# The last 128 columns of the last tile, stored as two transfers of 64 rows from two queues

## The chip, the cores and the metric

The kernel runs on one core of a Trainium2 chip. The core's engines are TensorE (PE, with its weight loads PEld), VectorE (DVE), ScalarE (ACT), GpSimd (POOL) and SyncE (SP); they run on their own and meet through semaphores. Sixteen DMA engines carry the transfers that SyncE and ScalarE issue here, each from a queue of its own (q1 and q10 in the profile). The metric is the device time of one execution in microseconds.

## The reference

One mixer block: a layer norm and a first product with GELU, a shift of the four quarters of its columns by one or two rows of the sequence, a second product, a residual, then a second layer norm and a two-layer MLP with another residual.

```python
B, S, D, F = 1, 2048, 512, 1792          # all inputs bfloat16
def reference(x, w1, w2, w3, w4):
    h = _gelu(_layernorm(x, axis=-1) @ w1)
    c = D // 4
    g0 = jnp.pad(h[:, :, 0*c:1*c], ((0, 0), (1, 0), (0, 0)))[:, :S, :]
    g1 = jnp.pad(h[:, :, 1*c:2*c], ((0, 0), (0, 1), (0, 0)))[:, 1:, :]
    g2 = jnp.pad(h[:, :, 2*c:3*c], ((0, 0), (2, 0), (0, 0)))[:, :S, :]
    g3 = jnp.pad(h[:, :, 3*c:   ], ((0, 0), (0, 2), (0, 0)))[:, 2:, :]
    hs = jnp.concatenate([g0, g1, g2, g3], axis=-1) @ w2
    x1 = x + hs
    h2 = _gelu(_layernorm(x1, axis=-1) @ w3) @ w4
    return x1 + h2
```

## The kernel before

The 2,048 rows of the sequence are held as 16 tiles of 128 rows, one row of a tile per partition: row 16p + t is partition p of tile t, so one partition's part of the output is 16 rows that follow each other, and one tile's store writes 128 pieces that lie 16 rows apart. Everything stays on chip between the two layers.

Operations are recorded one by one with `add(engine, name, function, reads, writes, dma)`. `arrange` then orders them: each engine has a list of names that come first, written out by hand, and all others follow in the order in which they were recorded. `emit` walks the ordered operations, works out for each which semaphores it must wait for, and gives every DMA a semaphore of its own that it raises by 16 when it has landed. At the end of SyncE's program it waits for every store (the operations whose names begin with `out`), line 168 and 169. When the program is built, these waits are put together two to an instruction, and one that is left over is held by the branch that ends SyncE's part (L92).

The first layer and the mixing (L357 to L494) take about the first 48 us, with a first part of the second layer's products (L526) among them. In the second layer the tiles go in four groups of four: `block3` (L502, with GELU on ScalarE, L513) makes the hidden activations of a group, and `m4` (L545) multiplies one tile of 128 rows by `w4`, 14 matmuls one after the other into one PSUM bank. `fin` (L553) adds the residual on VectorE (L557) into `o_sb`, a ring of four output tiles, and issues the store (L561), on SyncE unless told otherwise. Group 1 is computed ahead of group 0's second product, and so on, so that the last stretch is the second products of groups 2 and 3: eight tiles, and nothing but these.

The last tile (line 760) is cut in two by columns: 384 columns into bank 0 with a store on SyncE, then 128 columns into bank 7 with a store on ScalarE. ScalarE has no other work in this stretch: the slices of the page show it idle over the last 20 us and more. The last store's chain is thus: last matmul, addition of 128 x 128 on VectorE, issue on ScalarE's queue, transfer of 128 pieces of 256 B, landing, the wait on SyncE, and the barrier of all engines at the end.

Four helpers in the same function, `nbias_op`, `norm_act`, `negmean` and `norm_pool`, are not called by anything that runs: the only call stands behind `if t in ():` (line 624), which is never true. The two small tensors that they use, `nmean` and `nbias`, are allocated.

Of the kernel before, what the change touches and what calls it, by code (L numbers as in the profile page):

```python
# [5 lines left out]
P = 128  # L6
ACT_F = mybir.ActivationFunctionType
ALU = mybir.AluOpType
BF16 = mybir.dt.bfloat16
F32 = mybir.dt.float32  # L10
# [16 lines left out]
class Program:  # L27
# [7 lines left out]
    def add(self, eng, name, fn, reads=(), writes=(), dma=False):  # L35
        self.ops.append(Op(name, eng, fn, reads, writes, dma))
# [135 lines left out]
def bass_standalone__mixer_s_mlp__prompt_kernel(nc: bass.Bass, x, w1, w2, w3, w4, out):  # L172
    B, S, D = x.shape
    F = w3.shape[1]
    assert (B, S, D, F) == (1, 2048, 512, 1792)
    NT = S // P
# [7 lines left out]
    od = out[0].rearrange("(p t) d -> p t d", t=NT)  # L184
    ORDER = [(t + R + 2) % NT for t in range(NT)]
    POS = {t: k for k, t in enumerate(ORDER)}

    with ExitStack() as es:
        sb = lambda name, shape, dt: es.enter_context(nc.sbuf_tensor(name, shape, dt))
# [17 lines left out]
        st9 = sb("st9", [P, 2 * NT, 9], F32)  # L207
        mv = sb("mv", [P, 2 * NT, 2], F32)
        rstd = sb("rstd", [P, 2 * NT], F32)
        nmean = sb("nmean", [P, 2 * NT], F32)  # L210
        nbias = sb("nbias", [P, 2 * NT], F32)
        neghalf = sb("neghalf", [P, 4], F32)
        warm = sb("warm", [P, 1], F32)
        o_sb = sb("o_sb", [P, 4, D], BF16)
# [32 lines left out]
        add = pr.add  # L247
# [4 lines left out]
        def bres(b, n, tag):  # L252
            return [(("ps", b + i), tag) for i in range(n)]
# [28 lines left out]
        def src_of(layer, t):  # L282
            return (x_sb, ("x", t)) if layer == 0 else (x1_sb, ("x1", t))

        def dst_of(layer, t):
            return (xn, t, ("xn", t), 0) if layer == 0 else (x1n, POS[t] % 8, ("x1n", POS[t] % 8), t)
# [19 lines left out]
        def norm(layer, t):  # L306
            src, r = src_of(layer, t)
            dst, k, dr, tag = dst_of(layer, t)
            i = layer * NT + (t if layer == 0 else POS[t])
            add("dve", f"nm{layer}_{t}",  # L310
                lambda e: e.tensor_scalar(dst[:, k, :], src[:, t, :], mv[:, i, 0:1], rstd[:, i : i + 1],  # L311
                                          ALU.subtract, ALU.mult),
                reads=[(r, 0), (("mv", i), 0), (("rstd", i), 0)], writes=[(dr, tag)])

        def nbias_op(layer, t, n):
            i = layer * NT + (t if layer == 0 else POS[t])
            add("dve", f"nb{layer}_{t}",
                lambda e: e.scalar_tensor_tensor(nbias[:, i : i + n], mv[:, i : i + n, 0], -1.0,
                                                 rstd[:, i : i + n], ALU.mult, ALU.mult),
                reads=[(("mv", i + k), 0) for k in range(n)] + [(("rstd", i + k), 0) for k in range(n)],  # L320
                writes=[(("nb", i + k), 0) for k in range(n)])

        def norm_act(layer, t):
            src, r = src_of(layer, t)
            dst, k, dr, tag = dst_of(layer, t)
            i = layer * NT + (t if layer == 0 else POS[t])
            add("act", f"na{layer}_{t}",
                lambda e: e.activation(dst[:, k, :], src[:, t, :], ACT_F.Identity,
                                       bias=nbias[:, i : i + 1], scale=rstd[:, i : i + 1]),
                reads=[(r, 0), (("nb", i), 0), (("rstd", i), 0)], writes=[(dr, tag)])  # L330

        def negmean(layer, t, n):
            i = layer * NT + (t if layer == 0 else POS[t])
            add("dve", f"ng{layer}_{t}",
                lambda e: e.tensor_scalar(nmean[:, i : i + n], mv[:, i : i + n, 0], -1.0, None, ALU.mult),
                reads=[(("mv", i + k), 0) for k in range(n)], writes=[(("nmean", i + k), 0) for k in range(n)])

        def norm_pool(layer, t):
            src, r = src_of(layer, t)
            dst, k, dr, tag = dst_of(layer, t)  # L340
            i = layer * NT + (t if layer == 0 else POS[t])
            add("pool", f"np{layer}_{t}",
                lambda e: e.tensor_scalar(dst[:, k, :], src[:, t, :], nmean[:, i : i + 1], rstd[:, i : i + 1],
                                          ALU.add, ALU.mult),
                reads=[(r, 0), (("nmean", i), 0), (("rstd", i), 0)], writes=[(dr, tag)])


        def tp(t, n, b, raw):
# [192 lines left out]
        def m4(q, i, b, c0=0, c1=D, part=""):  # L541
            def f(e):
                ins = None
                for fc in range(FC):
                    ins = e.matmul(ps[:, 512 * b : 512 * b + c1 - c0], h2T[:, fc, q % 2, P * i : P * (i + 1)],  # L545
                                   w4_sb[:, fc, c0:c1], start=(fc == 0), stop=(fc == FC - 1))
                return ins

            add("pe", f"m4_{q}_{i}{part}", f,
                reads=[("w4", 0)] + [(("h2T", fc, q % 2, i // 2), q) for fc in range(FC)],  # L550
                writes=bres(b, 1, f"m4_{q}_{i}{part}"))

        def fin(q, i, b, c0=0, c1=D, part="", eng="sp"):  # L553
            k = 4 * q + i
            t = ORDER[k]
            add("dve", f"fin{t}{part}",
                lambda e: e.tensor_tensor(o_sb[:, k % 4, c0:c1], ps[:, 512 * b : 512 * b + c1 - c0],  # L557
                                          x1_sb[:, t, c0:c1], ALU.add),
                reads=bres(b, 1, f"m4_{q}_{i}{part}") + [(("x1", t), 0)], writes=[(("o", k % 4, c0), k)])
            add(eng, f"out{t}{part}",  # L560
                lambda e: e.dma_start(od[:, t, c0:c1], o_sb[:, k % 4, c0:c1]),  # L561
                reads=[(("o", k % 4, c0), k)], dma=True)

        def warmup(name, n, b):
            def f(e):
# [55 lines left out]
        for t in range(R, NT, 2):  # L621
            roots(0, t, 2)
        for t in range(R, NT):
            if t in ():
                nbias_op(0, t, 1)
                norm_act(0, t)
            else:
                norm(0, t)
        for t in range(R, NT, 2):
            if t in (8, 10):  # L630
                tp(t, 2, 6 + t // 2 % 2, False)
# [112 lines left out]
        for i, t in enumerate((0, 1, 2, 3, 4, 5, 6, 7)):  # L744
            b = (6, 7, 1)[i % 3]
# [3 lines left out]
        for i in range(4):  # L749
            m4(0, i, 6 + i % 2)  # L750
            fin(0, i, 6 + i % 2)
        block3(2)
        for i in range(4):
            m4(1, i, 6 + i % 2)
            fin(1, i, 6 + i % 2)
        block3(3)
        for q in (2, 3):
            for i in range(4):
                b = 6 + i % 2
                if (q, i) == (3, 3):  # L760
                    m4(q, i, 0, 0, 384, "a")
                    m4(q, i, 7, 384, 512, "b")
                    fin(q, i, 0, 0, 384, "a")
                    fin(q, i, 7, 384, 512, "b", eng="act")
                else:
                    m4(q, i, b)
                    fin(q, i, b)
# [32 lines left out]
```

## Time and profile before

| | us |
|---|---|
| median of three runs | 136.84 (136.6 to 136.96) |
| the profiled execution | 136.96 |
| its span in the profile | 134.9 |
| TensorE busy | 131.4 (97%) |
| VectorE busy | 58.0 (43%) |
| ScalarE busy | 46.7 (35%) |
| GpSimd busy | 12.5 (9%) |
| additions of `fin`, L557 | 17 of 0.66 on average |
| stores of 128 KB on SyncE, issue to landing | 15, median 1.8 |

The span runs from the first to the last instruction of the program; the execution's own time has some 2 us around it. The granted clock of TensorE is at full speed throughout. Busy shares are averages over the whole span: in the last 25 us TensorE works without a break, VectorE adds once per tile, ScalarE is idle, and the DMA engines move one store of 128 KB in about 3 us. A DMA's "issue" is the time that its instruction takes on the engine that issues it; its "landing" is when the sixteenth step of its semaphore arrives.

### The profile page before, as it was taken

How to read it: one execution, taken by the hardware profiler on the slowest of the kernel's cores; microseconds unless marked ns; L12 is line 12 of the kernel's file. 1: busy time of each engine (PE TensorE's matmuls, PEld its weight loads, DVE VectorE, ACT ScalarE, POOL GpSimd, SP SyncE). 2: the span in 40 equal slices, each digit the busy share in tenths (PEclk: the TensorE clock that was granted, in tenths of full speed). 3: DMA queues.
4: the chain of work that ended last, by engine and by line, in shares of the span. 5: the costliest groups of instructions: out<-in, count | busy, mean ns of one | idle time of the engine just before them, and what ended most of it. 6: DMA issues, size and time to landing. Idle time of an engine off the chain costs nothing.

```text
span 134.9 us, 1809 instructions
## 1 busy us (share of the span) xinstructions
PE 131.4 (97%) x729; PEld 69.5 (52%) x729; DVE 58.0 (43%) x135; ACT 46.7 (35%) x56; POOL 12.5 (9%) x25
## 2 busy tenths in 40 slices
PE   7989999999999999999999999999999999999993
PEld 2346866668885444444444444444444444444452
DVE  0399999799966786772222000122200002322222
ACT  3467871607963025551000555200066630000000
POOL 2024422220321012220000000000000000000000
PEclk9999999999999999999999999999999999999999
DMA  4998569985455993444112000011110001111121
GB/s 116 311 234 171 184 128 236 266 274 114 77 110 106 261 306 67 88 80 78 39 50 67 5 0 0 0 39 39 39 39 5 0 0 39 39 39 39 41 76 43
DMA packets 24568, 12.96 MB, mean 96 GB/s; under 512 B 16752, under 2 KB 23920, under 8 KB 24560
## 3 DMA queue, kind: packets, MB, share of 16 engines
q1 hardware_dynamic: 23984, 12.42, 36.0%
q10 hardware_dynamic: 576, 0.43, 1.1%
q8 instruction: 6, 0.10, 0.3%
q14 instruction: 2, 0.02, 0.1%
HBM read 6.82 MB, written 2.10 MB: 66 GB/s over the span
## 4 chain that ended last, share of the span: by engine, by line
PE 93%; DMA 3%; SPq 2%; issue 0%; DVE 0%
PE ps L545 36%; PE ps L502 27%; PE ps L526 9%; PE ps L444 6%; PE ps L484 5%; PE ps L470 5%; PE ps L412 3%; DMA x_sb<-in_x_dram 3%; PE ps L357 1%; SPq L274 1%; SPq L576 1%; DVE o_sb L557 0%; PE ps L400 0%
## 5 line engine op out<-in xcount | busy, mean ns | idle before, releaser
L545 PE MATMUL ps<-w_sb,h2T 128*128 128x512 bf16 (+2 forms) x238 | 48.9, 366 | 0.0
L557 DVE TENSOR_TENSOR o_sb<-ps,x_sb 128x512 bf16<-128x512 f32 (+2 forms) x17 | 11.2, 660 | 61.2 <-PE ps L545 61.2
L513 ACT ACTIVATE h2T<-ps 128x1024 bf16<-128x1024 f32 x21 | 21.5, 1023 | 46.2 <-PE ps L502 46.2
L502 PE MATMUL ps<-x1nT,w_sb 128*128 128x512 bf16 x168 | 36.7, 379 | 0.0
L545 PEld LDWEIGHTS ps<-w_sb,h2T 128*128 128x128 bf16 x238 | 22.8, 98 | 25.9
L502 PEld LDWEIGHTS ps<-x1nT,w_sb 128*128 128x128 bf16 x168 | 16.4, 98 | 19.8
L291 DVE BATCH_NORM_STATS2 st<-x_sb 128x6 f32<-128x512 bf16 x32 | 20.7, 679 | 4.6 <-DMA x_sb<-in_x_dram 4.5
L302 POOL TENSOR_TENSOR rstd<-mv,neghalf 128x2 f32<-128x2 f32 x16 | 11.6, 726 | 46.5 <-DVE mv L296 46.5
L526 PE MATMUL ps<-x1nT,w_sb 128*128 128x256 bf16 x112 | 12.4, 273 | 0.0
L526 PEld LDWEIGHTS ps<-x1nT,w_sb 128*128 128x128 bf16 x112 | 11.0, 98 | 1.5
L494 DVE TENSOR_TENSOR x_sb<-ps,x_sb 128x512 bf16<-128x512 f32 x16 | 10.6, 686 | 2.5 <-PE ps L470 1.5
L444 PE MATMUL ps<-xnT,w_sb 128*128 128x256 bf16 x80 | 9.2, 273 | 0.0
L537 ACT ACTIVATE h2T<-ps 128x1024 bf16<-128x1024 f32 (+1 forms) x8 | 7.1, 914 | 6.0 <-PE ps L526 6.0
L444 PEld LDWEIGHTS ps<-xnT,w_sb 128*128 128x128 bf16 x80 | 7.7, 98 | 1.2
L311 DVE TENSOR_SCALAR x1n<-x_sb,mv,rstd 128x512 bf16<-128x512 bf16 x16 | 5.9, 410 | 5.3 <-POOL rstd L302 5.3
L484 PE MATMUL ps<-w_sb,hTf 128*128 128x512 bf16 x32 | 7.2, 379 | 0.0
L470 PE MATMUL ps<-w_sb,hTf 128*128 128x512 bf16 x32 | 7.1, 379 | 0.0
L412 PE MATMUL ps<-w_sb,xnT 128*128 128x512 bf16 x24 | 6.0, 386 | 0.0
L454 ACT ACTIVATE hTf<-ps 128x1024 bf16<-128x1024 f32 x4 | 4.1, 1023 | 4.1 <-PE ps L444 4.1
L366 ACT ACTIVATE xnT<-ps 128x512 bf16<-128x512 bf16 (+1 forms) x6 | 4.4, 737 | 2.9 <-PE ps L357 2.9
L296 DVE BATCH_NORM_AGGREGATE mv<-st 128x2 f32<-128x9 f32 x32 | 5.0, 186 | 0.0
L470 PEld LDWEIGHTS ps<-w_sb,hTf 128*128 128x128 bf16 x32 | 3.1, 98 | 3.6
(28 smaller groups left out, 36.7 us busy)
## 6 DMA issues: line engine op xcount, KB each, us to landing
out_dram<-o_sb SPq DMA_DIRECT2D x15, 128.0 KB, 1.8
w_sb<-in_w_dram SPq DMA_DIRECT2D x1, 1792.0 KB, 7.8
x_sb<-in_x_dram SPq DMA_DIRECT2D x13, 128.0 KB, 3.4
w_sb<-in_w_dram SPq DMA_DIRECT2D x4, 256.0 KB, 4.2
w_sb<-in_w_dram SPq DMA_DIRECT2D x6, 128.0 KB, 3.1
w_sb<-in_w_dram SPq DMA_DIRECT2D x4, 192.0 KB, 3.5
w_sb<-in_w_dram ACTq DMA_DIRECT2D x2, 128.0 KB, 3.3
x_sb<-in_x_dram SPq DMA_DIRECT2D x1, 256.0 KB, 4.3
```

What stands on the lines that cost most here:

```text
L291: add("dve", f"st{layer}_{t}", lambda e: e.bn_stats(st9[:, i, 0:6], src[:, t, :]), reads=[(r, 0)], writes=[(("st6", i), 0)])
L302: lambda e: e.tensor_tensor(rstd[:, i : i + n], mv[:, i : i + n, 1], neghalf[:, 0:n], ALU.pow),
L412: ins = e.matmul(bank(b), xnT[:, t, c, :], w1_sb[:, c, :], start=(c == 0), stop=(c == DC - 1))
L444: ins = e.matmul(dst, w1_sb[:, c, P * fc : P * (fc + 1)], xnT[:, t : t + 2, c, :], start=(c == 0), stop=(c == DC - 1))
L470: ins = e.matmul(bank(b), hTf[:, c0 : c0 + P], w2_sb[:, j, :], start=(j == 0), stop=(j == DC - 1))
L484: ins = e.matmul(bank(b), hTf[:, w[0] : w[0] + P], w2_sb[:, j, :], start=first and n == 0, stop=last and n == len(js) - 1)
L494: lambda e: e.tensor_tensor(x1_sb[:, t, :], bank(b), x_sb[:, t, :], ALU.add),
L502: ins = e.matmul(bank(b), w3_sb[:, c, P * fc : P * (fc + 1)], x1nT[:, 4 * q : 4 * q + 4, c, :], start=(c == 0), stop=(c == DC - 1))
L513: lambda e: e.activation(h2T[:, fc : fc + 2, q % 2, :], src, ACT_F.Gelu_apprx_tanh),
L526: ins = e.matmul(dst, w3_sb[:, c, P * (fc + i) : P * (fc + i + 1)], x1nT[:, t : t + 2, c, :], start=(c == 0), stop=(c == DC - 1))
L545: ins = e.matmul(ps[:, 512 * b : 512 * b + c1 - c0], h2T[:, fc, q % 2, P * i : P * (i + 1)], w4_sb[:, fc, c0:c1], start=(fc == 0), stop=(f ...
L557: lambda e: e.tensor_tensor(o_sb[:, k % 4, c0:c1], ps[:, 512 * b : 512 * b + c1 - c0], x1_sb[:, t, c0:c1], ALU.add),
```

## The change

`fin` takes a tuple of engines in place of one. For n engines it records n stores, each of 128 / n partitions of the same columns, on the engines in turn, all behind the same addition. The calls that gave no engine give `("sp",)` by default and make one store as before. The last call, for 128 columns of the last tile, gives `("act", "sp")`: partitions 0 to 63 are stored from ScalarE's queue, 64 to 127 from SyncE's. The stores are 18 in place of 17, so SyncE has one semaphore more to wait for at the end. The four unused helpers, their tensors and the branch that is never taken are removed.

```diff
-        nmean = sb("nmean", [P, 2 * NT], F32)
-        nbias = sb("nbias", [P, 2 * NT], F32)
...
-        def nbias_op(layer, t, n):
...
-        def norm_act(layer, t):
...
-        def negmean(layer, t, n):
...
-        def norm_pool(layer, t):
...
-        def fin(q, i, b, c0=0, c1=D, part="", eng="sp"):
+        def fin(q, i, b, c0=0, c1=D, part="", eng=("sp",)):
             k = 4 * q + i
             t = ORDER[k]
             add("dve", f"fin{t}{part}",
                 lambda e: e.tensor_tensor(o_sb[:, k % 4, c0:c1], ps[:, 512 * b : 512 * b + c1 - c0],
                                           x1_sb[:, t, c0:c1], ALU.add),
                 reads=bres(b, 1, f"m4_{q}_{i}{part}") + [(("x1", t), 0)], writes=[(("o", k % 4, c0), k)])
-            add(eng, f"out{t}{part}",
-                lambda e: e.dma_start(od[:, t, c0:c1], o_sb[:, k % 4, c0:c1]),
-                reads=[(("o", k % 4, c0), k)], dma=True)
+            for n, e in enumerate(eng):
+                p0, p1 = P * n // len(eng), P * (n + 1) // len(eng)
+                add(e, f"out{t}{part}{n}",
+                    (lambda p0, p1: lambda e: e.dma_start(od[p0:p1, t, c0:c1], o_sb[p0:p1, k % 4, c0:c1]))(p0, p1),
+                    reads=[(("o", k % 4, c0), k)], dma=True)
...
-            if t in ():
-                nbias_op(0, t, 1)
-                norm_act(0, t)
-            else:
-                norm(0, t)
+            norm(0, t)
...
-                    fin(q, i, 7, 384, 512, "b", eng="act")
+                    fin(q, i, 7, 384, 512, "b", eng=("act", "sp"))
```

More of the change, by code (lines that the diff above doesn't have):

```diff
@@ L313, in norm @@
                 reads=[(r, 0), (("mv", i), 0), (("rstd", i), 0)], writes=[(dr, tag)])
-        def nbias_op(layer, t, n):
[L316 to L321, printed above, removed]
-        def norm_act(layer, t):
[L324 to L330, printed above, removed]
-        def negmean(layer, t, n):
[L333 to L336, printed above, removed]
-        def norm_pool(layer, t):
[L339 to L345, printed above, removed]
         def tp(t, n, b, raw):
```

## The prediction

> **What bounds the kernel now.** I read the chain of waits first, then the timeline of the last three microseconds, then the same stretch cut into windows with the share of the DMA engines.
>
> ```profile
> span 134.9 us, 1809 instructions
> PE 93%; DMA 3%; SPq 2%; issue 0%; DVE 0%
> ```
>
> TensorE carries 93% of the chain that ended last, in one piece from the first transposes to the last matmul. Nothing in the diff is an instruction of TensorE, so only what follows its last matmul can move. The timeline from 131.9 us (start, length, engine and line):
>
> ```profile
> 131.69 0.89 PE L545 MATMUL ps<-w_sb,h2T 128*128 128x128 bf16 x13
> 131.84 0.56 DVE L557 TENSOR_TENSOR o_sb<-ps,x_sb 128x384 bf16<-128x384 f32 x1 [1.58 <-PE ps L545]
> 132.42 0.33 SPq L561 DMA_DIRECT2D out_dram<-o_sb  x1
> 132.62 0.29 DVE L557 TENSOR_TENSOR o_sb<-ps,x_sb 128x128 bf16<-128x128 f32 x1 [0.22 <-PE ps L545]
> 132.94 0.35 ACTq L561 DMA_DIRECT2D out_dram<-o_sb  x1
> ```
>
> The reader is to see the order: matmuls end at 132.58, the last addition runs 132.62 to 132.91, ScalarE issues the last store at 132.94, and SyncE has been free since 132.75. The windows of the tail (stretch, length, busy per engine, then clock, DMA share, GB/s) show what that store does next:
>
> ```profile
> 133.70:133.79 0.09, 0.00 (x0) 0.00 (x0) 0.00 (x0) 0.00 (x0) 0.00 (x0) 1.00 0.00 0
> 133.79:134.07 0.28, 0.00 (x0) 0.00 (x0) 0.00 (x0) 0.00 (x0) 0.00 (x0) 1.00 0.55 117
> 134.07:134.42 0.35, 0.00 (x0) 0.00 (x0) 0.00 (x0) 0.00 (x0) 0.00 (x0) 1.00 0.00 0
> 134.42:134.88 0.46, 0.00 (x0) 0.00 (x0) 0.00 (x0) 0.00 (x0) 0.00 (x0) 1.00 0.00 0
> ```
>
> So of the 1.94 us from the issue to the end of the span, 0.85 us pass before the first packet (132.94 to 133.79), 0.28 us move data, 0.35 us pass from the last packet to the landing, and 0.46 us are SyncE's last waits and the closing barrier. Rows of the DMA view by size, and the packets of ScalarE's queue (q10) after 132.9 us:
>
> ```profile
> out_dram<-o_sb SPq DMA_DIRECT2D x15, 128.0 KB, 1.8
> out_dram<-o_sb SPq DMA_DIRECT2D x1, 96.0 KB, 1.7
> out_dram<-o_sb ACTq DMA_DIRECT2D x1, 32.0 KB, 1.5
> q10 hardware_dynamic: 144, 0.03, 7.4%
> ```
>
> Four times the bytes add only 0.3 us to a landing. The 144 packets are 128 rows of 256 B and 16 small ones, one for each DMA engine. The final waits, from the view of L169 before and after 134.05:
>
> ```profile
> L169 SPq EVENT_SEMAPHORE  x6: 28/28/28, 132.8 to 133.1; - x6
> L169 SPq EVENT_SEMAPHORE  x2: 28/28/28, 134.1 to 134.4; - x2
> ```
>
> Each of these waits holds for two stores. Six of them, long satisfied, take 0.3 us for five steps, so 0.06 us each; the seventh waits for the 96 KB store, the eighth for the last one, and the seventeenth store's is held by the branch behind them (L92).
>
> **The change part by part.** *Removed code.* Four helper functions and a branch that is never taken go, with two small tensors: 2 x 32 x 4 B = 256 B per partition. The instructions of TensorE, VectorE and GpSimd are the same in number, form and order, so I put this at 0.00 us. No cover is needed, since no instruction goes.
>
> *Issue on ScalarE.* Its store has 64 rows in place of 128, still behind the same addition, so it starts at 132.94. The duration does not follow the rows: the 1,792 KB load on SyncE takes 0.58 us for 1,792 runs of 1 KB, the stores 0.33 for 128. I take 0.35 us as before, 0.00 in the sum.
>
> *Issue on SyncE.* One more issue, which waits for the same addition. Queued behind it on SyncE are only the final waits, and only the closing barrier waits for those. SyncE ended its 96 KB issue at 132.75; six loads issued back to back from 2.12 us take 2.80 us together and the last of them 0.43, so (2.80 - 0.43) / 5 = 0.47 us from start to start, and it could start again at 132.42 + 0.47 = 132.89, ahead of 132.91. It starts with ScalarE's, at about 132.93, and ends at 133.27. Its early waits then run from about 133.3 to 133.7 (six of 0.06 us), still ahead of the landing of the 96 KB store at 134.08, where SyncE stops today too. So 0.00, hidden by that flight; without the cover the 0.33 us would stand in front of the end.
>
> *From issue to first packet.* SyncE's 96 KB store takes 0.83 us (132.42 to 133.25), ScalarE's 0.85. What the trace of the tail doesn't show is two issues at one moment. The only such pair opens the kernel:
>
> ```profile
> 0.74 0.39 SPq L274 DMA_DIRECT2D x_sb<-in_x_dram  x1
> 0.74 0.89 ACTq L576 DMA_DIRECT2D w_sb<-in_w_dram  x2
> ```
>
> In the trace's packet records SyncE's queue moves its first packet at 1.77 us, 1.03 after its issue, and ScalarE's at 2.04, 1.30 after. Bounds for the later half: 0.00 (the tail's own rows) to 1.30 - 0.85 = +0.45. The pair is two reads of 128 KB at a cold start, the tail's are writes of a quarter of that or less, so I take 0.00 and keep +0.45 for the range.
>
> *Data.* The 128 rows of 256 B are spread as before over the 16 engines, 4 + 4 for each in place of 8, and 32 small packets stand in place of 16. Busy share 0.55 of 0.28 us is 0.15 us for each engine, so its engines start one after the other within the rest, about 0.13 us. If the two queues halve both parts, 0.28 becomes 0.14: -0.14. If they only interleave on the same engines: 0.00, with one more small packet of at most 0.01. By size (0.3 us for 96 KB more) 16 KB less would be worth 0.3 x 16/96 = 0.05. I take 0.00, since both halves end on the same engines, and keep -0.14 and +0.01.
>
> The Trainium skill, DMA: Bandwidth & Descriptors, section Rules for kernel authors, advises against just this: two transfers to disjoint partition halves share the same 16 engines and serialize, and one of 128 partitions is to be used. By that rule the gain of 0.14 is not there; by the size row alone it would be 0.05. The trace of before has no pair of halves that would decide.
>
> *Landing.* 0.35 us from the last packet, one row, taken unchanged: 0.00. The fifteen full stores land within 0.1 us of each other but for one of 2.3 us, which had an instruction fetch on one engine at 130.5; none is near the last store.
>
> *One more final wait.* Seventeen stores become eighteen: the first wait is now for one store alone, then eight pairs, then the branch. The last two event waits are for SyncE's half and for ScalarE's half. When both land together, the second is passed 0.06 us after the first where today only one stands there: +0.06. SyncE's first packet comes 0.02 us sooner after its issue, so its half lands sooner by about that and I take 0.06 - 0.02 = +0.04. Bounds: 0.00 (it lands 0.06 ahead) and +0.06.
>
> *Sum.* 0.00 + 0.00 + 0.00 + 0.00 + 0.04 = +0.04 us: a span of 134.88 + 0.04 = 134.92, and 136.96 + 0.04 = 137.00 for the profiled execution, whose own time of 136.96 has 2.08 us around the span. It is the slowest of the three runs shown, 0.12 above the median of 136.84, so the forecast for the median is 136.88, **136.9**. Differences under 0.3%, 0.41 us, are about what a measurement of this kernel cannot tell from no change: the three runs alone spread over 0.36.
>
> **The rivals.** *The halves run side by side.* Data 0.28 to 0.14, the extra wait +0.04: 136.84 - 0.14 + 0.04 = 136.74. For it: two queues, and engines that now start one after the other within 0.28 us. Against it: each queue's 64 rows go over all 16 engines. It can't reach far: even with no data at all, 0.85 + 0.35 of 1.48 us stay, a gain of 0.28 at most (136.56).
>
> *The two issues hold each other up before their first packets* (slower). The place is the 0.85 us between issue and first packet, the price that of the kernel's first pair, 0.45 us for ScalarE's queue: 136.84 + 0.45 = 137.29; SyncE's half is then long landed and the extra wait costs nothing. It decides for "slower" from 0.41 us. For it: in that pair ScalarE's first packet comes 0.27 us after SyncE's though both were issued at 0.74. Against it: both are late there, as a cold start would make them, and 0.27 alone (137.1) would not show.
>
> *SyncE comes late*, so the halves aren't issued together. An issue after a wait can take 0.58 us (the 1,792 KB load) in place of 0.33: a half later by 0.25 us, 136.84 + 0.25 = 137.09. Against it: all sixteen stores on SyncE took 0.33 to 0.36, and each had waited too.
>
> **How the numbers follow.** Interleaved halves with an extra wait 0.57 (136.9), side by side 0.17 (136.7), held up 0.20 (137.1 to 137.3), SyncE late 0.06 (137.1). Slower by over 0.41 us: the upper end of held up, 0.13, and 0.03 from the scatter of a median of a few runs on the others, 0.16 in all. Faster by over 0.41 lies beyond the floor of 0.28, so it needs scatter: 0.07. Within: 0.77. The range runs from 136.5 (the floor of 136.56 less some scatter) to 137.3 (held up at its full price); about 15 in 100 lie outside.
>
> **What would show it.** Right: two issues of 64 rows at 132.93 to 132.95 against 132.94 for one, both queues' packets within one stretch of about 0.28 us that begins 0.85 after, both landings within 0.05 us, nine final waits in place of eight, with the last two 0.06 apart, and the matmuls ending at the same distance from the start. Held up: a gap between the first packets of q1 and q10, or both over 0.9 us after their issues. Side by side: a stretch of 0.14 us. Wrong altogether: a shift ahead of 132.9 us, an instruction fetch in the tail, or a landing over 0.5 us after the last packet.

## The result and the profile after

The changed kernel is slower: a median of 137.46 us against 136.84, a ratio of 1.0044 (95% interval 1.0029 to 1.0058), so between 0.40 and 0.79 us slower. Its profiled execution took 137.32 us, with a span of 135.13. The head of its page and its chain:

```profile
span 135.1 us, 1811 instructions
PE 89%; SPq 4%; DMA 2%; DVE 2%; issue 0%
```

The two new instructions are one store and one final wait. TensorE's smaller share of the chain is a difference in the first 12 us, where the chain now goes by SyncE's loads and a layer norm's statistics, and it cost nothing: the long run of TensorE behind it begins 0.35 us earlier than in the profiled execution of before (the first block of 32 matmuls at 14.55 us against 14.90), and so do the last additions. That much differs between executions (in the profiles shown here the last addition ends between 132.5 and 133.3 us), so I compare the tail, from the end of the last addition to the end of the span. Before it was 134.88 - 132.91 = 1.97 us. The timeline after (start, length, engine and line):

```profile
131.49 0.56 DVE L523 TENSOR_TENSOR o_sb<-ps,x_sb 128x384 bf16<-128x384 f32 x1 [1.58 <-PE ps L511]
132.07 1.07 SPq L529 DMA_DIRECT2D out_dram<-o_sb  x2
132.27 0.29 DVE L523 TENSOR_TENSOR o_sb<-ps,x_sb 128x128 bf16<-128x128 f32 x1 [0.22 <-PE ps L511]
132.59 0.56 ACTq L529 DMA_DIRECT2D out_dram<-o_sb  x1
```

The addition ends at 132.56, so the tail is 135.13 - 132.56 = 2.57 us, 0.60 longer; the medians differ by 0.62. All of the change in time is behind the last addition. ScalarE's issue takes 0.56 us in place of 0.35. SyncE's row merges two issues: 0.33 for 384 columns and, from 132.59, 0.56 for the half. The windows of the tail, with the DMA share and GB/s at the end of a line, then the issues and the packets after 132.5 us:

```profile
133.36:133.78 0.42, 0.00 (x0) 0.00 (x0) 0.00 (x0) 0.00 (x0) 0.00 (x0) 1.00 0.00 0
133.78:134.30 0.52, 0.00 (x0) 0.00 (x0) 0.00 (x0) 0.00 (x0) 0.00 (x0) 1.00 0.38 63
134.30:134.68 0.38, 0.00 (x0) 0.00 (x0) 0.00 (x0) 0.00 (x0) 0.00 (x0) 1.00 0.00 0
134.68:135.14 0.46, 0.00 (x0) 0.00 (x0) 0.00 (x0) 0.00 (x0) 0.00 (x0) 1.00 0.00 0
```

```profile
q1 hardware_dynamic: 224, 0.11, 16.4%
q10 hardware_dynamic: 80, 0.02, 3.9%
issues: line engine op xcount, KB each, median us to landing
out_dram<-o_sb SPq DMA_DIRECT2D x1, 16.0 KB, 1.8
out_dram<-o_sb ACTq DMA_DIRECT2D x1, 16.0 KB, 2.1
```

The two halves land 1.8 and 2.1 us after their issues; the whole took 1.5. The first packet comes 133.79 - 132.59 = 1.20 us after the start of the issues, and the stretch with data is 0.52 us long in place of 0.28. In the packet records SyncE's 64 rows run from 133.79 to 134.02 and ScalarE's from 134.06 to 134.30: one queue after the other, not between each other. The final waits before and after 133.7 us:

```profile
L169 SPq EVENT_SEMAPHORE  x6: 17/28/28, 133.2 to 133.5; - x6
L169 SPq EVENT_SEMAPHORE  x3: 28/28/28, 133.7 to 134.7; - x3
```

Nine waits, six of them early and over by 133.55, as forecast. The last one starts when ScalarE's half has landed (134.67), and from there to the end it is 0.46 us, as before.

### The profile page after: what moved, and what is told of

Same layout as the page of the kernel before. It is cut to its first block, busy times and chain, and to the rows that moved or that the text cites. A ratio compares the mean times of both kernels' runs of the same rounds, so it can differ in the third digit from the quotient of the medians.

```text
span 135.1 us, 1811 instructions
## 1 busy us (share of the span) xinstructions
PE 131.2 (97%) x729; PEld 69.1 (51%) x729; DVE 58.0 (43%) x135; ACT 46.8 (35%) x56; POOL 12.5 (9%) x25
## 4 chain that ended last, share of the span: by engine, by line
PE 89%; SPq 4%; DMA 2%; DVE 2%; issue 0%
PE ps L511 36%; PE ps L468 27%; PE ps L492 9%; PE ps L410 6%; PE ps L436 5%; PE ps L450 5%; DMA x_sb<-in_x_dram 2%; SPq L272 2%; SPq L351 1%; DVE st L289 1%; PE ps L323 1%; SPq L544 1%; DVE xn L309 0%; DVE o_sb L523 0%
```

## The experiments

Each was made from the changed kernel. "Tail" is as above, from each one's profile; ratios are to the kernel before, run on the same chip. "First packet" is read from the packet records, counted from the issue's start.

**One whole store again.**

```diff
-                    fin(q, i, 7, 384, 512, "b", eng=("act", "sp"))
+                    fin(q, i, 7, 384, 512, "b", eng=("act",))
```

> The changed kernel with its last store whole again (128 rows on ScalarE's queue); the removed helpers and tensors stay removed. Theory (two issues at one moment hold each other up): the tail, from the end of the last addition to the end of the span, is 1.97 us as before (2.57 in the changed kernel), the issue 0.35, and the median is that of before, 136.8 to 136.9. Rival (the removed tensors or the new line numbers matter): the median stays near 137.46.

The tail is 1.96 us, the median 136.66, the ratio 0.9991 (0.9979 to 1.0004). The timeline and the issue:

```profile
132.52 0.35 ACTq L529 DMA_DIRECT2D out_dram<-o_sb  x1
```

The removed helpers and tensors are worth nothing that can be measured; the loss is in the split of one store.

**One half alone.**

```diff
             for n, e in enumerate(eng):
                 p0, p1 = P * n // len(eng), P * (n + 1) // len(eng)
+                if e is None:
+                    continue
...
-                    fin(q, i, 7, 384, 512, "b", eng=("act", "sp"))
+                    fin(q, i, 7, 384, 512, "b", eng=("act", None))
```

> Leaves out the store of rows 64 to 127 of the last 128 columns; ScalarE's store of rows 0 to 63 stays and no other is issued at its moment. Theory (simultaneous issues): issue 0.35 us, first packet 0.85 after it, tail 1.9 to 1.97 us, median 136.8. Rival (a transfer of 64 rows is slow by itself): issue 0.56, first packet 1.2 or more, tail 2.3 or more, median 137.2 or more.

The rival held. With no other issue at its moment the half still takes 0.54 us to issue, and its first packet comes after 1.18 us in place of 0.85. Timeline, then its landing:

```profile
132.93 0.54 ACTq L531 DMA_DIRECT2D out_dram<-o_sb  x1
```

```profile
out_dram<-o_sb ACTq DMA_DIRECT2D x1, 16.0 KB, 1.8
```

Tail 2.26 us, 0.29 more than before; median 137.25, ratio 1.0028 (1.0013 to 1.0042). About half of the loss is a price of the transfer of 64 rows itself.

**Halves by columns.**

```diff
-                p0, p1 = P * n // len(eng), P * (n + 1) // len(eng)
+                a0, a1 = c0 + (c1 - c0) * n // len(eng), c0 + (c1 - c0) * (n + 1) // len(eng)
                 add(e, f"out{t}{part}{n}",
-                    (lambda p0, p1: lambda e: e.dma_start(od[p0:p1, t, c0:c1], o_sb[p0:p1, k % 4, c0:c1]))(p0, p1),
+                    (lambda a0, a1: lambda e: e.dma_start(od[:, t, a0:a1], o_sb[:, k % 4, a0:a1]))(a0, a1),
```

> The last 128 columns as two stores of 128 rows x 64 columns, from ScalarE and SyncE at the same moment. Theory (simultaneous issues, whatever the rows): issues 0.56 us each, the first packets of the two queues 0.27 apart, tail 2.57 to 2.7 us, median 137.4 to 137.6. Rival (64 rows are slow): issues 0.33 and 0.35, tail 2.0 us, median 136.9.

Neither. Two issues at one moment, of 128 rows each, take 0.33 and 0.37 us (0.85 in SyncE's row are two issues 0.52 apart):

```profile
132.29 0.85 SPq L529 DMA_DIRECT2D out_dram<-o_sb  x2
...
132.82 0.37 ACTq L529 DMA_DIRECT2D out_dram<-o_sb  x1
```

```profile
out_dram<-o_sb SPq DMA_DIRECT2D x1, 16.0 KB, 1.4
out_dram<-o_sb ACTq DMA_DIRECT2D x1, 16.0 KB, 1.6
```

SyncE's half lands a little sooner than the whole (1.4 against 1.5), ScalarE's later: its first packet 0.06 us later, and 0.49 us in place of 0.35 from its last packet to its landing. Tail 2.11, 0.14 more than before; median 137.03, ratio 1.0016 (1.0005 to 1.0026). So two transfers issued at one moment have a price of their own, and my theory had put all of the loss on it.

**Which queue, or which rows.**

```diff
-                    fin(q, i, 7, 384, 512, "b", eng=("act", "sp"))
+                    fin(q, i, 7, 384, 512, "b", eng=("sp", "act"))
```

> Two halves of 64 rows at one moment, but SyncE stores rows 0 to 63 and ScalarE rows 64 to 127. Theory: as the changed kernel, issues 0.56 us, one queue's first packet 0.27 after the other's, tail 2.57, median 137.4 to 137.5; which queue comes second does not follow the rows. Rival (the rows decide, through the partitions that are read): rows 64 to 127 come first as in the changed kernel, so now ScalarE's queue is first.

Tail 2.58 us, median 137.26, ratio 1.0037 (1.0021 to 1.0053). SyncE's half is again the first (landing 1.8 us after its issue) and ScalarE's the second (2.1), its first packet 0.28 us after SyncE's. SyncE's issue starts 0.005 us ahead of ScalarE's in both kernels. The rows don't decide.

**Every tile in halves of 64 rows.** The same pair at the end, and fifteen pairs in the body, where matmuls hide them.

```diff
-            fin(0, i, 6 + i % 2)
+            fin(0, i, 6 + i % 2, eng=("act", "sp"))
...
-            fin(1, i, 6 + i % 2)
+            fin(1, i, 6 + i % 2, eng=("act", "sp"))
...
-                    fin(q, i, b)
+                    fin(q, i, b, eng=("act", "sp"))
```

> Every output tile, not only the last part, is stored as two halves of 64 rows from ScalarE and SyncE at one moment: fifteen pairs hidden behind matmuls, and the pair at the end as in the changed kernel. Theory (a transfer of 64 rows costs its issue and its start each time): all issues about 0.55 us, the first packets of the two queues about 0.27 apart in every pair, the tail 2.57 us, the median 137.4. Rival (only the first transfer of a new shape on a queue is slow): the first pair 0.55, the later ones 0.33 to 0.37, the tail 2.0 to 2.15, the median about 137.0.

The issues in the view by line (shortest, median, longest in ns; SyncE's shortest is the store of 384 columns):

```profile
L529 SPq DMA_DIRECT2D out_dram<-o_sb x17: 366/467/557, 63.9 to 133.0; - x17
L529 ACTq DMA_DIRECT2D out_dram<-o_sb x16: 497/498/557, 63.9 to 133.0; - x16
```

Both had a part of it. The first pair takes 0.557 us on each queue, all later ones 0.467 and 0.498, so 0.06 to 0.09 is paid only once; the rest is paid each time. The first packets of the two queues are 0.28 to 0.30 us apart (issue to first packet 1.12 on SyncE, 1.42 on ScalarE) in every later pair, for rows of 1 KB and of 256 B alike. So the second queue doesn't wait for the end of the first one's data: with rows of 1 KB SyncE's data last 0.46 to 0.47 us, and ScalarE's packets begin before they end. The tail is 2.89 us, which here holds something else: 0.89 us lie behind the last landing in place of 0.46. The waits and the branch behind them:

```profile
L169 SPq EVENT_SEMAPHORE  x16: 28/28/28, 133.5 to 135.0; - x16
L92 SPq COMPARE_BRANCH  x1: 38/38/38, 135.5 to 135.5; - x1
```

The waits don't make the difference: all but the last are over when the last half lands (134.97), and the last starts 0.02 us later. But the branch starts only 0.49 us after the last wait, 0.07 in the changed kernel, though the store that it waits for had landed at 65.9. The median, 137.47, ratio 1.0037 (1.0017 to 1.0057), can therefore not be read against the changed kernel's; the packets can.

**Every tile in halves of columns.** The edit of the column halves with that of the run before.

> As the run before, but the parts of every pair are 128 rows by half of the columns, at the end too. Theory (two issues at one moment cost little where each has 128 rows): issues 0.33 and 0.35 to 0.38 us, ScalarE's first packets 0.06 to 0.1 after SyncE's, ScalarE's landing 0.1 to 0.2 later than alone, tail 2.11, median 137.0. Rival (the shared engines make the second of two wait for the first one's data): the second queue's first packet comes later the wider the rows are, over 0.2 us after the first queue's in the body's pairs of 256 columns.

Issues 0.33 and 0.37 us as expected. ScalarE's first packet comes 0.17 us after SyncE's for rows of 512 B (0.12 in the first pair) and 0.08 for the 128 B at the end, so the second queue does wait longer behind wider rows, though not 0.2. ScalarE's landings are 0.16 us later than SyncE's. Tail 2.48, of which 0.87 are behind the last landing, with the same late branch as in the run before; median 137.27, ratio 1.0019 (1.0003 to 1.0035).

**Other numbers of rows, one transfer at a time.**

```diff
+            cuts = [0, (64, 32, 96, 16, 112, 64, 32, 96, 16, 112, 64, 32, 96, 16, 112)[k], P] if len(eng) == 2 else [0, P]
             for n, e in enumerate(eng):
-                p0, p1 = P * n // len(eng), P * (n + 1) // len(eng)
+                p0, p1 = cuts[n], cuts[n + 1]
...
-            fin(0, i, 6 + i % 2)
+            fin(0, i, 6 + i % 2, eng=("sp", "sp"))
...
-            fin(1, i, 6 + i % 2)
+            fin(1, i, 6 + i % 2, eng=("sp", "sp"))
...
-                    fin(q, i, 7, 384, 512, "b", eng=("act", "sp"))
+                    fin(q, i, 7, 384, 512, "b", eng=("act",))
...
-                    fin(q, i, b)
+                    fin(q, i, b, eng=("sp", "sp"))
```

> Every output tile but the last is stored by two transfers of SyncE, one behind the other, of r and 128 - r rows with r = 64, 32, 96, 16, 112 in turn, three times; the last store is whole on ScalarE. Theory (128 rows are cheap, anything less is dear): every part's issue is 0.53 us or more, the same for all r. Rival (by the number of rows): the issue grows or falls steadily from 16 to 112 rows. Second rival (first of a shape only): the three turns differ, the first being slow.

None of the three. The first parts of the second turn, in the timeline, are 64, 32, 96, 16 and 112 rows; those of the third turn take the same to 0.01 us:

```profile
91.06 0.47 SPq L530 DMA_DIRECT2D out_dram<-o_sb  x1
...
94.08 0.32 SPq L530 DMA_DIRECT2D out_dram<-o_sb  x1
...
97.11 0.32 SPq L530 DMA_DIRECT2D out_dram<-o_sb  x1
...
112.21 0.31 SPq L530 DMA_DIRECT2D out_dram<-o_sb  x1
115.23 0.32 SPq L530 DMA_DIRECT2D out_dram<-o_sb  x1
```

Only 64 rows are dear: issue 0.47 and first packet after 1.12 us, the others 0.31 to 0.32 and 0.81, even a little less than 128 rows (0.33 and 0.83). The second parts say the same: a 64-row part right behind another takes 0.59 to 0.60, all others 0.42 to 0.43 but for one of 1.36 at 130.7 us, while a fetch of instructions was in flight (130.5 to 131.7).

**Both halves on ScalarE.**

```diff
-                    fin(q, i, 7, 384, 512, "b", eng=("act", "sp"))
+                    fin(q, i, 7, 384, 512, "b", eng=("act", "act"))
```

> The two halves of 64 rows of the last 128 columns both on ScalarE's queue, one issue behind the other, none at the same moment. Theory (64 rows are dear, and a second issue adds its own length): issues 0.53 us each, the second half starts 0.55 to 0.6 after the first, tail 2.26 + 0.55 = 2.8 us, median 137.6 to 137.7. Rival (the two queues at one moment are what costs): issues 0.35 and 0.45, tail 1.97 + 0.45 = 2.4, median 137.3.

```profile
133.36 1.18 ACTq L529 DMA_DIRECT2D out_dram<-o_sb  x2
```

The theory held, with a tail 0.14 us longer than it said: two issues of 0.54 and 0.60 us, the second 0.57 after the first; tail 2.94, median 137.71, ratio 1.006 (1.0034 to 1.0085). In the tail the split is worse still without a second queue (2.94 against 2.57); the intervals of the two ratios overlap.

**Cut at row 96.**

```diff
-                p0, p1 = P * n // len(eng), P * (n + 1) // len(eng)
+                p0, p1 = ((0, 96), (96, P))[n] if len(eng) == 2 else (0, P)
```

> The last 128 columns as two stores at one moment, as in the changed kernel, but cut at row 96: 96 rows from ScalarE, 32 from SyncE. Theory (64 rows are what is dear, and two issues at one moment add some 0.14 us): issues 0.31 to 0.40 us, first packets 0.81 to 0.95 after them, tail 2.05 to 2.2 us, median 0.1 to 0.2 above before. Rival (any cut of the rows is dear where the two are issued at one moment): issues 0.5 us or more, tail 2.4 or more, median 0.4 or more above before.

```profile
132.41 0.86 SPq L529 DMA_DIRECT2D out_dram<-o_sb  x2
...
132.93 0.38 ACTq L529 DMA_DIRECT2D out_dram<-o_sb  x1
```

The theory held. The same split into two row blocks on two queues at one moment, 32 rows further down: issues of 0.35 and 0.38 us, first packets 0.84 and 0.88 after them, tail 2.08, median 136.93, ratio 1.0007 (0.9991 to 1.0024). Four fifths of the changed kernel's loss in the tail (0.49 of 0.60) are gone.

**Less behind the landing.** The whole last store on SyncE, 384 columns on ScalarE, and the waits for old stores moved ahead.

```diff
-                    fin(q, i, 0, 0, 384, "a")
-                    fin(q, i, 7, 384, 512, "b", eng=("act", "sp"))
+                    fin(q, i, 0, 0, 384, "a", eng=("act",))
+                    fin(q, i, 7, 384, 512, "b", eng=("sp",))
...
+            tail = [op for op in self.ops if op.eng == "sp"][-2]
...
+                    if op is tail:
+                        for s in outs[:14]:
+                            objs[e].wait_ge(sems[s], 16)
+                        del outs[:14]
...
-                for s in outs:
+                for s in outs[::-1]:
```

> One whole last store again, but on SyncE, with the store of 384 columns on ScalarE; the waits for the first fourteen stores stand ahead of the fifteenth store's issue, and the branch at the end of SyncE's part waits for the last store itself. Theory (the tail is issue, start, data, landing and what SyncE does after the landing): SyncE's first packet 0.02 us sooner and one wait of 0.07 less behind the landing, tail 1.88 us against 1.97, median 0.1 below before, which the timing can hardly tell. Rival (the time behind the landing is the barrier's alone): tail 1.95 to 1.97.

Tail 1.915 us, 0.05 less than before and not the 0.09 expected: the landing came 0.02 sooner, and 0.44 us in place of 0.46 lie behind it. Median 136.85, ratio 0.9988 (0.9973 to 1.0004): no difference that the timing shows.

**Counts that share out as four rows to an engine.** The tuple of the run with other numbers of rows becomes (48, 56, 60, 40, 24), three times.

> As the run with r of 64, 32, 96, 16 and 112 rows, with r = 48, 56, 60, 40 and 24 in turn, three times; 128 - r rows follow each. Theory (64 rows alone are dear, as a count): every first part's issue is 0.31 to 0.34 us once warm and its first packet 0.80 to 0.83 after it. Rival (four rows to a DMA engine are dear: 64 rows gave 16 engines four rows each; 56, 60 and 40 rows can be shared out as four rows to 14, 15 and 10): the first parts of 56, 60 and 40 rows take 0.47 or more, those of 48 and 24 do not.

The first parts of 48, 56, 60, 40 and 24 rows take 0.32, 0.33, 0.33, 0.29 and 0.30 us, with first packets after 0.76 to 0.81. For 56, 60 and 40 rows the landing's semaphore rises in 15, 16 and 11 steps, one of them soon after the issue (0.45 to 0.5 us after its start, ahead of any data, which starts at 0.76 to 0.81) and 14, 15 and 10 as the rows land: so many engines, with four rows each. Four rows to an engine are not dear either. The Trainium skill, DMA: Bandwidth & Descriptors, section Why a DMA increments its semaphore by 16 and not by 1, has the issuing sequencer add the steps of the engines that a transfer does not use; these steps agree with it.

## Why the prediction was wrong

The forecast was 136.9 in a range of 136.5 to 137.3; 137.46 was measured. The direction was carried by the rival called held up, with its place right and its price too small. The tail by terms, in us, from the issue on ScalarE; the middle column is the run with one half alone:

| term | before | 64 rows alone | changed |
|---|---|---|---|
| issue to ScalarE's first packet | 0.85 | 1.18 | 1.46 |
| its data | 0.27 | 0.23 | 0.24 |
| last packet to landing | 0.35 | 0.35 | 0.38 |
| landing to the end | 0.46 | 0.46 | 0.46 |

*The step that failed is "Issue on ScalarE"*, with its sentence that the duration does not follow the rows, and "From issue to first packet" that rests on it. The row behind it was a load of 1,792 runs against stores of 128: it showed that the time grows far less than the rows, and nothing of 64. A transfer of 64 rows alone has its first packet 1.18 - 0.85 = 0.33 us later, 0.18 of it in the issue (0.535 against 0.353) and 0.15 behind it, which makes the tail 0.29 longer. I had no row of fewer than 128 partitions for a plain store, and should have said so and bounded it.

*From issue to first packet, two at one moment.* Taken at 0.00 with 0.45 as its bound. Measured are 1.46 - 1.18 = 0.28 us on top of the 64 rows, close to the 0.27 by which the kernel's first two transfers follow each other, the row that I set aside as a cold start. With halves by columns, 128 rows each, it is only 0.06. The bound of 0.45 did not hold for the two together (1.46 - 0.85 = 0.61): I had bounded only this one cause, and that is why the time lies above the range.

*Issue on SyncE.* It did start at ScalarE's moment, and its early waits were covered, as forecast; it took 0.56 us in place of 0.33.

*Data.* 0.00 came close (0.24 for the later half against 0.27), for another reason: the halves neither ran side by side nor interleaved, they followed each other. The Trainium skill's rule of the halves that serialize (DMA: Bandwidth & Descriptors, Rules for kernel authors) agrees with the trace in that nothing is gained: 0.23 + 0.24 us of data in a row. It doesn't tell of a loss, and the tail lost 0.60.

*One more final wait.* Put at 0.04, measured at 0.00: ScalarE's half lands 0.30 us after SyncE's, so the wait for SyncE's was long passed, as the rival had it. *Landing* (0.35 to 0.38) and *removed code* (ratio 0.9991) were right. The floor of the side-by-side case was never near.

What stays open is why 64 rows, of eleven counts tried, are the only dear one, and what the two queues share that lets the second one's packets begin later. No run issues the two halves some time apart on two queues, so whether the delay needs the same moment is not shown either. The runs show where the time is, not what does it.

## What to carry to other kernels

A small last store costs issue, start and landing, not bytes: of its 1.47 us here only 0.27 are data. Splitting it over two queues took nothing off that in any of the cuts tried here, and it adds the second queue's delay. Where a part of the tile's partitions has to be stored, measure that count by itself: here 96 and 32 rows were cheap and 64 were not.

## What the runs showed that was not expected

- A transfer of 64 rows takes 0.47 us to issue and 1.12 to its first packet each time; 16, 24, 32, 40, 48, 56, 60, 96, 112 and 128 rows take 0.29 to 0.33 and 0.76 to 0.84 (SyncE's queue, single or first parts, after the first two tiles).
- The first 64-row transfer on a queue takes another 0.06 to 0.09 us to issue (0.557 against 0.467 and 0.498).
- Of two stores issued at one moment, SyncE's, which starts 0.005 us ahead, came first in every pair, and ScalarE's packets 0.27 to 0.30 us later with 64 rows, 0.08 to 0.18 with 128.
- Where every tile is stored as a pair, 0.87 to 0.89 us lie behind the last landing in place of 0.46, and the difference is one gap of 0.47 to 0.49 us between SyncE's last wait and its branch (0.07 before and after). The number of waits doesn't explain it: with other numbers of rows there are 16 too, and there the branch starts 0.07 us after the last wait, while a gap of 0.49 stands between the second and the third wait, where the flight of the last store covers it. What makes the gap no run shows.
